# wq loaded ahead of the transposes, and k and q of each tile in turn, in a gated mix of linear attention and a GeGLU FFN

## The chip, the cores and the metric

The kernel runs on one core of one Trainium2 chip. The metric is the device time of one execution in microseconds (us). A profiled execution also leaves a trace, whose span, from the first to the last instruction, is 1.2 to 1.5 us shorter than the time in nearly every run. SP and ACT name the queues of SyncE and ScalarE, from which the loads are issued. "Landing" below is the moment at which the last of the 16 DMA engines reports a load complete, read from the trace's landing records.

## The reference, cut to what matters

S = 2048 rows, D = 640, F = 1728, 32 heads of 20.

```python
g = sigmoid((x * gate_w).sum(-1, keepdims=True))
q, k, v = split(x @ wqkv)                        # 32 heads of 20
pq, pk = phi(q), phi(k)                          # phi(t) = where(t > 0, t + 1, exp(t)) + 1e-6
kv, z = einsum(pk, v), pk summed over the rows
a = (pq @ kv) / (pq @ z + 1e-6) @ wo
b = (gelu(x @ w_gate) * (x @ w_up)) @ w_down
out = g * a + (1 - g) * b
```

The change touches only the K/Q stage at the start: k = x wk and q = x wq for 16 tiles of 128 rows, followed by phi. A unit below is the k or the q of one tile: five pairs of matmuls (512 and 128 columns), one pair for each 128-row chunk of the weight (wk0 to wk4 are the chunks of wk, x0 and x1 the first tiles of x). The stage has 32 units, that is 160 pairs. After it comes the product of pk with x, "the pk^T x stage", then the FFN and the output, none of which the change touches.

## The kernel before

x is needed transposed. The first three tiles are loaded plainly and transposed on TensorE (T); the other 13 come through DMA transposes. `P.op` records an operation with what it reads and writes, and semaphore waits follow from that. `seq` gives the order of the units; `slot(n)` gives each unit a pair of PSUM banks (`ps` in the lines of the profile, where the matmuls write) in turn, four pairs in all.

```python
NXN, KLEAD = 3, 7
load_x(0, "sp");  load_wk(0, "act"); load_wk(1, "sp"); load_x(1, "act"); load_x(2, "sp")
load_wk(2, "act"); load_wk(3, "sp"); load_wk(4, "act"); # ... gate weights on "act"
for i in range(NXN, NT):
    if i == KLEAD:
        dma_in(wq[:, :, 0:640], ...)             # all of wq, behind four transposes
    load_xT(i, after=([r_wk[1]] if i == NXN else ()))
# ...
seq = [("k", i) for i in range(KLEAD)] + [("q", 0)]
for i in range(KLEAD, NT):
    seq += [("q", i - KLEAD + 1), ("k", i)]
seq += [("q", i) for i in range(NT - KLEAD + 1, NT)]
# ...
warm(6, 512)                                     # matmuls on constants, to warm the array
T(0, [0], 7); T(0, [1, 2, 3, 4], 6)              # transposes of tile 0, copied back by VectorE
KM(0, [0]); T(1, [0, 1, 2, 3, 4], 7); KM(0, [1]); warm(2, 128)
KM(1, [0]); KM(1, [1]); T(2, [0, 1, 2, 3, 4], 6)
# ... chunk 2 of k0 and k1, chunks 0 to 2 of k2; gate_col() transposes the gate weights
for k in range(3, KC):
    for n in range(3):
        KM(n, [k])                               # three k tiles by chunk
for n in range(2 * NT):                          # the rest, unit by unit
    if seq[n][0] == "q": QM(n)
    elif n >= 3:         KM(n, list(range(KC)))
    phi1(n); phi2(n)                             # Exp on ScalarE, two VectorE operations
```

## Time and profile before

| | before |
|---|---|
| time, median of 3 runs | 276.66 us (276.47 to 277.04) |
| span of the trace | 275.2 us |
| PE busy | 271.3 us, 99% of the span |
| first transpose | 4.17 us |
| first k product | 4.72 us |
| first q product | 16.08 us |
| first product of the pk^T x stage | 50.11 us |

From the page of the kernel before: the busy time of TensorE (first its matmuls, then its weight loads, VectorE and ScalarE), the array's clock in 40 slices, and the chain of work that ended last.

```profile
PE 271.3 (99%) x1694; PEld 139.3 (51%) x1694; DVE 138.8 (50%) x234; ACT 78.3 (28%) x132; POOL 26.1 (9%) x28
...
PEclk9999999999999999999999999999999999999999
...
PE 96%; DMA 1%; DVE 1%; ACT 0%; issue 0%
```

TensorE bounds the kernel almost from end to end, so what a new order of loads and tiles can win lies in its first microseconds. The chain of waits cut off at 20 us shows them, as start, length and what (lines that are plain runs of matmuls are left out):

```profile
0.81 3.32 DMA pool<-in_A_x_dram
...
4.44 0.24 DVE pool L419
...
5.49 0.50 DVE pool L419
...
10.02 0.71 ACT pool L462
10.75 0.34 DVE pool L472
11.12 0.84 DVE pool L476
```

The chain begins with the load of x tile 0, then alternates between TensorE and VectorE's copies of transposes, and at 10 us passes once through phi of unit 0: unit 4 needs the banks of unit 0. The timeline of TensorE gives the rate (start, duration, engine, line, operation, and in brackets the idle time before and what ended it):

```profile
0.84 2.72 PE L401 MATMUL ps<-const-bfloat16-1.0 128*128 128x512 bf16 x6 [0.84 <-PEq L818]
4.17 0.45 PE L415 MATMUL ps<-pool 128*128 128x128 bf16 x5 [0.61 <-DMA pool<-in_A_x_dram]
4.72 0.39 PE L438 MATMUL ps<-pool 128*128 128x512 bf16 x1
4.95 0.22 PE L439 MATMUL ps<-pool 128*128 128x128 bf16 x1
...
16.08 0.38 PE L453 MATMUL ps<-pool 128*128 128x512 bf16 x1
```

Two speeds are to be seen. The six warm matmuls of 512 columns take 0.43 us each (start to start); from 4.17 us on a pair of 512 and 128 columns takes 0.39 and 0.22 us, overlapping, and in a row a pair starts every 0.272 us.

### The profile page before, as it was taken

What the parts mean: (1) busy time and instruction counts of PE and PEld (TensorE: products, weight loads), DVE (VectorE), ACT (ScalarE), POOL (GpSimd) and SP (SyncE); (2) the same over time, 40 slices, a digit from 0 to 9 for tenths busy, and PEclk for the clock granted to TensorE, in tenths of its full rate; (3) what the DMA queues carried; (4) which work ended last, traced back from release to release, by engine and by line L of the source; (5) the groups of instructions that cost most, each with busy time, mean ns of one, the idle gap of its engine ahead of it and who ended that gap; (6) DMA issues with size and microseconds to landing.
All of it is one profiled execution on the core that took longest, in us unless ns stands there. A gap on an engine that the chain in (4) does not pass through costs nothing.

```text
span 275.2 us, 4067 instructions
## 1 busy us (share of the span) xinstructions
PE 271.3 (99%) x1694; PEld 139.3 (51%) x1694; DVE 138.8 (50%) x234; ACT 78.3 (28%) x132; POOL 26.1 (9%) x28
## 2 busy tenths in 40 slices
PE   7999999999999999999999999999999999999997
PEld 3555555555545444444444444444555555555553
DVE  1598888510234324999999999535100122212223
ACT  1455555210421454223322223224555100000000
POOL 5000000000000401242433422000000000000000
PEclk9999999999999999999999999999999999999999
DMA  6797999001121111122121231380000011111111
GB/s 206 164 181 176 388 403 311 15 11 39 24 48 22 50 46 53 26 46 48 26 49 24 48 45 29 67 304 14 0 0 2 15 42 40 48 50 48 50 40 55
DMA packets 36400, 22.38 MB, mean 81 GB/s; under 512 B 25759, under 2 KB 34975, under 8 KB 36383
## 3 DMA queue, kind: packets, MB, share of 16 engines
q1 hardware_dynamic: 35797, 21.47, 28.3%
q10 hardware_dynamic: 586, 0.66, 0.8%
q8 instruction: 13, 0.21, 0.3%
q14 instruction: 4, 0.03, 0.0%
HBM read 13.11 MB, written 2.62 MB: 57 GB/s over the span
## 4 chain that ended last, share of the span: by engine, by line
PE 96%; DMA 1%; DVE 1%; ACT 0%; issue 0%
PE ps L623 41%; PE ps L766 20%; PE ps L530 6%; PE ps L729 6%; PE ps L453 6%; PE ps L438 6%; PE ps L454 2%; PE ps L532 2%; PE ps L730 2%; PE ps L598 2%; PE ps L439 1%; DMA pool<-in_A_x_dram 1%; PE ps L750 1%; PE ps L644 1%; PE ps L660 1%; DVE pool L777 0%
## 5 line engine op out<-in xcount | busy, mean ns | idle before, releaser
L623 PE MATMUL ps<-pool 128*128 128x512 bf16 x520 | 113.7, 379 | 0.0
L623 PEld LDWEIGHTS ps<-pool 128*128 128x128 bf16 x520 | 50.4, 98 | 60.0 <-issue 0.3
L766 PE MATMUL ps<-pool 128*128 128x512 bf16 (+1 forms) x416 | 57.2, 299 | 0.0
L631 DVE TENSOR_TENSOR pool<-ps,pool 128x512 bf16<-128x512 f32 x52 | 35.8, 688 | 33.5 <-PE ps L623 30.4
L629 ACT ACTIVATE pool<-ps 128x512 f32<-128x512 f32 x52 | 31.1, 597 | 72.5 <-PE ps L623 72.5
L777 DVE SCALAR_TENSOR_TENSOR pool<-ps,pool 128x512 bf16<-128x512 f32 (+1 forms) x32 | 16.2, 547 | 63.8 <-PE ps L766 63.8
L766 PEld LDWEIGHTS ps<-pool 128*128 128x128 bf16 x416 | 31.9, 98 | 25.2 <-issue 1.1
L675 POOL TENSOR_TENSOR pool<-pool 128x640 f32<-128x640 bf16 x16 | 22.5, 1408 | 139.7 <-DMA pool<-z_row 86.6
L462 ACT ACTIVATE pool<-ps 128x640 bf16<-128x640 f32 x32 | 22.3, 704 | 23.2 <-PE ps L439 13.0
L476 DVE SCALAR_TENSOR_TENSOR pool<-ps,pool 128x640 bf16<-128x640 f32 x32 | 26.4, 825 | 2.2
L438 PE MATMUL ps<-pool 128*128 128x512 bf16 x80 | 23.5, 380 | 0.5 <-DVE pool L419 0.2
L683 DVE TENSOR_TENSOR pool<-pool 128x640 bf16<-128x640 bf16 x16 | 23.0, 1440 | 0.6
L453 PE MATMUL ps<-pool 128*128 128x512 bf16 x80 | 22.9, 379 | 0.0
L530 PE MATMUL ps<-pool 128*128 128x512 bf16 x80 | 21.9, 379 | 0.0
L729 PE MATMUL ps<-pool 128*128 128x512 bf16 x80 | 21.8, 379 | 0.0
L454 PE MATMUL ps<-pool 128*128 128x129 bf16 x80 | 17.6, 220 | 0.0
L532 PE MATMUL ps<-pool 128*128 128x129 bf16 x80 | 17.6, 220 | 0.0
L439 PE MATMUL ps<-pool 128*128 128x128 bf16 x80 | 17.5, 219 | 0.0
L730 PE MATMUL ps<-pool 128*128 128x128 bf16 x80 | 17.5, 219 | 0.0
L734 ACT ACTIVATE pool<-ps,pool 128x640 f32<-128x640 f32 x16 | 12.7, 794 | 9.2 <-PE ps L730 9.2
L677 DVE TENSOR_REDUCE pool<-pool 128x32 f32<-128x640 f32 x16 | 13.0, 810 | 0.0
L438 PEld LDWEIGHTS ps<-pool 128*128 128x128 bf16 x80 | 7.8, 98 | 10.1 <-DVE pool L419 1.0
(51 smaller groups left out, 125.7 us busy)
## 6 DMA issues: line engine op xcount, KB each, us to landing
out_dram<-pool SPq DMA_DIRECT2D x15, 160.0 KB, 1.8
pool<-in_B_w_gate_dram SPq DMA_DIRECT2D x1, 2080.0 KB, 14.1
pool<-in_B_w_up_dram SPq DMA_DIRECT2D x1, 2080.0 KB, 18.8
pool<-in_A_wqkv_dram SPq DMA_DIRECT2D x2, 800.0 KB, 11.8
pool<-in_A_x_dram SPq DMA_DIRECT2D x1, 1280.0 KB, 8.7
pool<-in_B_w_down_dram SPq DMA_DIRECT2D x1, 1120.0 KB, 6.0
pool<-in_A_wo_dram SPq DMA_DIRECT2D x6, 160.0 KB, 9.0
pool<-in_B_w_down_dram SPq DMA_DIRECT2D x1, 960.0 KB, 8.1
```

Source lines behind the costliest of these rows:

```text
L438: e.matmul(ps[:, b0, :], lhs, wk[:, k, 0:512], start=(k == 0), stop=(k == KC - 1))
L453: e.matmul(ps[:, b0, :], lhs, wq[:, k, 0:512], start=(k == 0), stop=(k == KC - 1))
L454: last = e.matmul(ps[:, b1, 0:129], lhs, wq[:, k, 512:641], start=(k == 0), stop=(k == KC - 1))
L476: P.op("dve", lambda e: e.scalar_tensor_tensor(dst, ps_flat[:, b0 * 512:b0 * 512 + 640], 1.0 + EPS, e_buf[m], ALU.add, ALU.max), reads=[ba ...
L530: e.matmul(ps[:, bs[n], :], lhs, x_aug[:, i, 0:512], start=(i == 0), stop=(i == NT - 1))
L532: last = e.matmul(ps[:, bt, n * 129:(n + 1) * 129], lhs, x_aug[:, i, 512:641], start=(i == 0 and n == 0), stop=(i == NT - 1), skip_group_c ...
L623: last = e.matmul(ps[:, b, :], w[:, k, fc * 128:(fc + 1) * 128], xT[:, k, j * 512:(j + 1) * 512], start=(k == 0), stop=(k == KC - 1))
L629: P.op("act", lambda e: e.activation(ge[n], ps[:, gb, :], ACT.Gelu_apprx_tanh), reads=[bank[gb]], writes=[r_ge[n]])
L631: P.op("dve", lambda e: e.tensor_tensor(hT[fc][:, j * 512:(j + 1) * 512], ps[:, ub, :], ge[n], ALU.mult), reads=[bank[ub], r_ge[n]], write ...
L729: e.matmul(ps[:, b0, :], lhs, w2[:, m, 0:512], start=(m == 0), stop=(m == KC - 1))
L730: last = e.matmul(ps[:, b1, 0:128], lhs, w2[:, m, 512:640], start=(m == 0), stop=(m == KC - 1))
L766: last = e.matmul(dst, lhs, wd[:, fc, c0:c0 + cn], start=False, stop=(fc == NFC - 2), skip_group_check=True)
```

## The change

The intent: have wq there early, so that q of a tile can follow its k at once and only two tiles need transposing on TensorE; let four units (k0, k1, q0, q1) consume the weights chunk by chunk as they land; then take k and q of each tile in turn, which needs a new transposed tile only every 2.7 us.

```diff
-NXN = 3
-KLEAD = 7
+NXN = 2
-            load_x(0, "sp"); load_wk(0, "act"); load_wk(1, "sp"); load_x(1, "act"); load_x(2, "sp")
-            load_wk(2, "act"); load_wk(3, "sp"); load_wk(4, "act"); gate weights on "act"
+            gate weights on "act"
+            load_x(0); load_wk(0); load_x(1, "act"); load_wk(1); load_wk(3)      # default queue: SP
+            P.op("act", lambda e: e.activation(eg[:, 0:1], zero, ACT.Exp), ...)  # early table load
+            load_wk(2, "act"); load_wk(4, "act")
+            load_wq(0, 2); load_wq(2, KC, "act")
             for i in range(NXN, NT):
-                if i == KLEAD: dma_in(wq[:, :, 0:640], ...)
-                load_xT(i, after=([r_wk[1]] if i == NXN else ()))
+                load_xT(i, after=([r_wk[4]] if i == NXN else ()))
 # ... (cut: resources of the two first tiles; QM takes a list of chunks)
+            seq = [("k", 0), ("k", 1), ("q", 0), ("q", 1)]
+            for i in range(2, NT):
+                seq += [("k", i), ("q", i)]
-            warm(6, 512) ... three tiles by chunk, as shown above
+            warm(5, 512); warm(1, 128)
+            T(0, [0], 7); T(0, [1, 2, 3, 4], 6); warm(3, 128); KM(0, [0])
+            T(1, [0], 7); T(1, [1, 2, 3, 4], 6); warm(3, 128); KM(1, [0])
+            for k in (1, 3): KM(0, [k]); KM(1, [k])
+            gate_col()
+            for k in (2, 4): KM(0, [k]); KM(1, [k])
+            # then q0 and q1 by chunk: QM(2, [k]); QM(3, [k]) for k = 0, 1, 2, then [3, 4]; then unit by unit
```

(The diff is cut, and lines are joined.)

More of the change, by code (lines that the diff above doesn't have):

```diff
@@ L300, in bass_gated_mix__linear_attn_block__geglu_ffn__prompt_kernel @@
             r_xT = [P.sb("xT%d" % i, R_XT, R_XT + KC * S) for i in range(NT)]
-            r_x0a = P.sb("x0a", R_XT, R_XT + 128)
+            r_xTa = [P.sb("xTa%d" % i, R_XT, R_XT + S) for i in range(NXN)]
             r_wk = [P.sb("wk%d" % k, R_WK + k * 640, R_WK + (k + 1) * 640) for k in range(KC)]
@@ L341, in load_wk, with load_x, load_wq @@
                 dma_in(wk[:, k, :], A_wqkv[k * 128:(k + 1) * 128, 640:1280], [r_wk[k]], eng=eng)
-            load_x(0, "sp")
-            load_wk(0, "act")
-            load_wk(1, "sp")
+            def load_x(i, eng="sp"):
+                dma_in(x_aug[:, i, 0:640], A_x[0, i * 128:(i + 1) * 128, :], [r_xn[i]], eng=eng)
+            def load_wk(k, eng="sp"):
+                dma_in(wk[:, k, :], A_wqkv[k * 128:(k + 1) * 128, 640:1280], [r_wk[k]], eng=eng)
+            def load_wq(k0, k1, eng="sp"):
+                dma_in(wq[:, k0:k1, 0:640],
+                       A_wqkv[k0 * 128:k1 * 128, 0:640].rearrange("(k p) w -> p k w", p=128),
+                       r_wq[k0:k1], eng=eng)
+            dma_in(gw_sb[0:5, :], gate_w.rearrange("(k p) -> k p", p=128), [r_gw], eng="act")
+            load_x(0)
+            load_wk(0)
             load_x(1, "act")
-            load_x(2, "sp")
+            load_wk(1)
+            load_wk(3)
+            zero = nc.const_aps.tensor(0.0, (128, 1), F32)
+            P.op("act", lambda e: e.activation(eg[:, 0:1], zero, ACT.Exp), writes=[r_eg[0]])
             load_wk(2, "act")
-            load_wk(3, "sp")
             load_wk(4, "act")
-            dma_in(gw_sb[0:5, :], gate_w.rearrange("(k p) -> k p", p=128), [r_gw], eng="act")
+            load_wq(0, 2)
+            load_wq(2, KC, "act")
             def load_xT(i, after=()):
@@ L358, in bass_gated_mix__linear_attn_block__geglu_ffn__prompt_kernel @@
             for i in range(NXN, NT):
-                if i == KLEAD:
-                    dma_in(wq[:, :, 0:640], A_wqkv[:, 0:640].rearrange("(k p) w -> p k w", p=128), r_wq)
-                load_xT(i, after=([r_wk[1]] if i == NXN else ()))
+                load_xT(i, after=([r_wk[4]] if i == NXN else ()))
             dma_in(x_aug[:, NXN:8, 0:640],
@@ L408, in slot @@
             def slot(n):
-                return SLOTS[n] if n < 3 else SLOTS[n % 4]
+                return SLOTS[n % 4]
             def T(i, ks, tb):
@@ L421, in T @@
                     psb[:, tb, 0:len(ks) * 128].rearrange("p (k s) -> p k s", k=len(ks))),
-                    reads=[bank[tb]], writes=[r_x0a if i == 0 and ks[0] == 0 else r_xT[i]])
-            seq = [("k", i) for i in range(KLEAD)] + [("q", 0)]
-            for i in range(KLEAD, NT):
-                seq += [("q", i - KLEAD + 1), ("k", i)]
-            seq += [("q", i) for i in range(NT - KLEAD + 1, NT)]
+                    reads=[bank[tb]], writes=[r_xTa[i] if ks[0] == 0 else r_xT[i]])
+            seq = [("k", 0), ("k", 1), ("q", 0), ("q", 1)]
+            for i in range(2, NT):
+                seq += [("k", i), ("q", i)]
             def KM(n, ks):
@@ L441, in fn, with QM @@
                     return last
-                P.op("pe", fn, reads=[r_x0a if i == 0 and ks == [0] else r_xT[i]] + [r_wk[k] for k in ks],
+                P.op("pe", fn, reads=[r_xTa[i] if i < NXN and ks == [0] else r_xT[i]] + [r_wk[k] for k in ks],
                      writes=[bank[b0], bank[b1]])
-            def QM(n):
+            def QM(n, ks):
                 i = seq[n][1]
@@ L450, in fn @@
                     last = None
-                    for k in range(KC):
+                    for k in ks:
                         lhs = xT[:, k, i * 128:(i + 1) * 128]
@@ L456, in fn @@
                     return last
-                P.op("pe", fn, reads=[r_xT[i], r_gcol] + r_wq, writes=[bank[b0], bank[b1]])
+                P.op("pe", fn, reads=[r_xT[i], r_gcol] + [r_wq[k] for k in ks],
+                     writes=[bank[b0], bank[b1]])
             def phi1(n):
@@ L485, in gate_col @@
                      reads=[bank[7]], writes=[r_gcol])
-            warm(6, 512)
+            ALLK = list(range(KC))
+            warm(5, 512)
+            warm(1, 128)
             T(0, [0], 7)
             T(0, [1, 2, 3, 4], 6)
+            warm(3, 128)
             KM(0, [0])
-            T(1, [0, 1, 2, 3, 4], 7)
-            KM(0, [1])
-            warm(2, 128)
+            T(1, [0], 7)
+            T(1, [1, 2, 3, 4], 6)
+            warm(3, 128)
             KM(1, [0])
-            KM(1, [1])
-            T(2, [0, 1, 2, 3, 4], 6)
-            KM(0, [2])
-            KM(1, [2])
-            KM(2, [0])
-            KM(2, [1])
-            KM(2, [2])
+            for k in (1, 3):
+                KM(0, [k])
+                KM(1, [k])
             gate_col()
-            for k in range(3, KC):
-                for n in range(3):
-                    KM(n, [k])
+            for k in (2, 4):
+                KM(0, [k])
+                KM(1, [k])
             for n in range(2 * NT):
-                if seq[n][0] == "q":
-                    QM(n)
-                elif n >= 3:
-                    KM(n, list(range(KC)))
+                if n == 2:
+                    for k in range(3):
+                        QM(2, [k])
+                        QM(3, [k])
+                    QM(2, [3, 4])
+                    QM(3, [3, 4])
+                elif n > 3:
+                    (KM if seq[n][0] == "k" else QM)(n, ALLK)
                 phi1(n)
                 phi2(n)
-                if n == 6:
+                if n == 8:
                     late_constants()
```

## The prediction

> **What bounds the kernel now.** TensorE. The page has PE busy 271.3 of 275.2 us, and the chain of waits is 96% PE. In the steady part of the K/Q stage a 512+128 matmul pair starts every 0.272 us (timeline); 160 such pairs are 43.6 us. The stage runs from the first transpose at 4.17 us, which waited for x tile 0 (0.61 us by the waits view), to the first pk^T x matmul at 50.11 us: 45.9 us. Only 2.4 us of it, plus the start before 4.17 us, can be won.
>
> Where the 2.4 us lie (timeline, 4.17 to 16.08 us, 35 pairs = 9.5 us of 11.9): transposes and the copy to the first product 0.55; transposes of tiles 1 and 2 and two warm matmuls about 0.8; holes at 5.8 to 6.0 and 7.4 to 7.7 us behind the copies of transposes; gate transpose 0.3; 0.34 before the fourth K tile at 12.00 us, which waits for the first phi to free its banks.
>
> **What the change does.**
> 1. x0 now is alone at the head of the SP queue; only a 1.2 KB load precedes x1 on ACT's. Before, x0 shared the engines with wk0 and landed at 3.9 to 4.1 us. [...]together they move about 360 KB per us here. Estimate: x0 (164 KB) lands at 3.4 to 3.8 us, saving 0.3 to 0.7 us.
> 2. One tile fewer by PE transpose: about 0.35 us of PE and one hole of 0.2 to 0.3 us saved. More small warm matmuls (seven of 128 instead of two) take 0.1 to 0.3 us back.
> 3. Four accumulators (k0, k1, q0, q1) run before a slot is needed again, so the 0.34 us bank wait goes.
> 4. Added: the early Exp pulls the table load (1.28 us) ahead of wk2 and wk4 on ACT; these land about 1 us later (estimate 6.0 and 7.0 us), which is why chunk 3 precedes 2. PE reaches chunk 2 at about 6.9, so at most 0.3 us of new wait.
> 5. wq (820 KB) ahead of the transposes: x0, x1, wk and wq are 1.97 MB, about 5.5 us at that rate; all landed by about 8.3 us, needed between 8.0 and 9.1. The DMA transposes wait for wk4, first issue about 7 instead of 4.84 us, first tile about 10.3 us (3.5 us from issue to landing before); needed at about 10.7. After that tiles arrive every 1.3 us and are used every 2.72, so no stall.
>
> **Sum.** Four units end at about 10.7 us, 28 more at 1.362 us each end at about 48.9 us: the pk^T x stage starts 1.2 us earlier on the PE chain. Allowing for small waits I take 1.1 us: 276.66 becomes **275.5 us** (-0.4%), 8 in 10 between 274.4 and 276.5. Chances: faster by over 2% 0.01, within 2% 0.98, slower by over 2% 0.01.
>
> **What would show it.** In the timeline: first transpose at 3.4 to 3.8 us; first pk^T x matmul at 48.6 to 49.5; no DVE wait near 12 us; no PE wait on DMA transposes; from there to the end both traces equal in length (225 us).
>
> **What would make it wrong.** x0 landing no earlier (gain about 0.6); wk2/wk4 landing after 7.5 us because ACT's table load holds its queue longer (PE stalls, up to 1 us, and the transposes start late behind it); the first DMA-transposed tile after 11 us; the array clock falling back to half rate in an early wait (the six warm matmuls took 0.45 us each).

("They" are the two queues: in the profile before, the core's DMA engines moved 387 KB from 3 to 4 us and 356 KB from 4 to 5 us. 10.7 and 28 times 1.362 us come to 48.8, put there as 48.9, 1.2 us before 50.11, of which 1.1 were taken.)

## The result, and the profile after

| | before | after |
|---|---|---|
| time, median of 6 runs each | 276.79 us (276.47 to 277.04) | 276.21 us (275.65 to 277.09) |
| ratio, 95% interval | | 0.9982 (0.9964 to 1.0001) |
| span of the trace | 275.2 us | 274.9 us |
| first transpose | 4.17 us | 3.12 us |
| first k product | 4.72 us | 4.49 us |
| first q product | 16.08 us | 9.01 us |
| first product of the pk^T x stage | 50.11 us | 49.82 us |

A ratio is the mean time of one kernel's fast runs over that of the other's of the same rounds, so it is not quite the ratio of the medians quoted. The gain is 0.2%, less than half of the predicted 0.4%. Two later jobs timed the same kernel again at 0.9986 (0.9974 to 0.9998) and 0.9977 (0.9964 to 0.9991): three jobs, 0.14 to 0.23%, that is 0.4 to 0.6 us in place of 1.1. The interval of the first job alone just includes no gain; those of the two later ones do not.

From the page after, the same lines:

```profile
PE 271.7 (99%) x1693; PEld 140.3 (51%) x1693; DVE 138.5 (50%) x234; ACT 78.5 (29%) x133; POOL 26.1 (9%) x28
...
PEclk9999999999999999999999999999999999999999
...
PE 97%; DMA 1%; DVE 0%; SPq 0%; issue 0%
```

The chain of waits up to 14 us, its first lines:

```profile
0.81 0.39 SPq L332
1.20 0.06 issue
1.26 3.10 DMA pool<-in_A_wqkv_dram
4.35 0.14 issue
4.49 0.59 PE ps L451
...
5.18 0.53 PE ps L429 x5
```

And TensorE's timeline:

```profile
0.84 2.40 PE L415 MATMUL ps<-const-bfloat16-1.0 128*128 128x512 bf16 x6 [0.84 <-PEq L836]
3.12 0.71 PE L429 MATMUL ps<-pool 128*128 128x128 bf16 x5
...
4.49 0.59 PE L451 MATMUL ps<-pool 128*128 128x512 bf16 x1 [0.34 <-DMA pool<-in_A_wqkv_dram]
4.87 0.31 PE L452 MATMUL ps<-pool 128*128 128x128 bf16 x1
...
5.83 0.63 PE L451 MATMUL ps<-pool 128*128 128x512 bf16 x1
...
6.69 0.22 PE L452 MATMUL ps<-pool 128*128 128x128 bf16 x1
6.74 0.38 PE L451 MATMUL ps<-pool 128*128 128x512 bf16 x1
...
7.76 0.39 PE L451 MATMUL ps<-pool 128*128 128x512 bf16 x1
...
8.59 0.38 PE L451 MATMUL ps<-pool 128*128 128x512 bf16 x1
8.80 0.22 PE L452 MATMUL ps<-pool 128*128 128x128 bf16 x1
9.01 0.38 PE L466 MATMUL ps<-pool 128*128 128x512 bf16 x1
```

Three things are to be seen. The chain no longer starts with x0 but with wk0, which landed at 4.35 us: x0 was there at 3.07 and the first transpose ran 1.05 us earlier than before, but the first product only 0.23 us earlier. Until 6.6 us the matmuls have the half-rate durations (0.59 to 0.63, 0.31, and 0.71 for five transposes, against 0.45). And between the last k product and the first q product there is a gap: the matmul of 512 columns before the last 128 one started at 8.59, a pair takes 0.272, so the q product was due at 8.86 and started at 9.01. The first part of wq (chunks 0 and 1) landed at 8.87.

From the first q product on nothing moves. Its distance to the pk^T x stage is 40.81 us, and from there the trace lasts 225.1 us as before (275.2 less 50.11, 274.9 less 49.82). So the question is why the first q product came at 9.01 us and not at 8.0: the prediction had four units end at 10.7 us, and q0 and q1 are ten pairs of 0.272 us, which puts their start at 8.0.

### The profile page after: what moved, and what is told of

It is laid out like the page before. It is cut to its first block, busy times and chain, and to the rows that moved or that the text cites. A ratio compares the mean times of both kernels' runs of the same rounds, so it can differ in the third digit from the quotient of the medians.

```text
span 274.9 us, 4067 instructions
## 1 busy us (share of the span) xinstructions
PE 271.7 (99%) x1693; PEld 140.3 (51%) x1693; DVE 138.5 (50%) x234; ACT 78.5 (29%) x133; POOL 26.1 (9%) x28
## 4 chain that ended last, share of the span: by engine, by line
PE 97%; DMA 1%; DVE 0%; SPq 0%; issue 0%
PE ps L641 41%; PE ps L784 20%; PE ps L451 7%; PE ps L466 6%; PE ps L747 6%; PE ps L548 6%; PE ps L452 2%; PE ps L550 2%; PE ps L467 2%; PE ps L748 2%; PE ps L616 2%; DMA pool<-in_A_wqkv_dram 1%; PE ps L768 1%; PE ps L662 1%; PE ps L678 1%; DVE pool L795 0%
## 5 line engine op out<-in xcount | busy, mean ns | idle before, releaser
L486 DVE TENSOR_SCALAR pool<-pool 128x640 bf16<-128x640 bf16 x32 | 10.4, 326 | 5.3 <-ACT pool L476 4.1
```

## The experiments

Two theories stood at the start. **Clock**: the array stayed at half rate up to 6.6 us, where the profile before had happened to be at full rate from 3.9 us. **Loads**: the products wait for wk0, x1 and wq, which land later than reckoned, whatever the clock. The key figures of all profiles are here, worked out from the timeline and the landing records. "Full rate" is where the durations change. The two intervals are from the issue of x0 to the first q product and to the first product of the pk^T x stage; x0 is issued at 0.80 or 0.81 us except in the runs named pw (pre-warmed: matmuls on constants run before the first load).

```
run            full rate  wk0 landed  wq, first part  first q   x0 issue to q   x0 issue to pk^T x
before            3.9        3.92        15.06         16.08       15.27            49.30
look_before_1     5.6        3.75        15.08         16.35       15.54            49.57
pw_before      before x0   x0+3.17     x0+14.33       21.29       15.00            49.03
after             6.6        4.35         8.87          9.01        8.20            49.01
look_after_1      5.0        3.98         9.51          9.65        8.85            49.66
after_again       6.5        4.54         8.71          8.93        8.13            48.95
after_3           6.8        3.90         8.62          8.76        7.96            48.77
pw_after       before x0   x0+3.04      x0+7.89        14.86        8.03            48.84
nowq            4.1-4.8       4.64          -            8.25        7.45            48.35
pw_nowq        before x0   x0+4.20         -           15.18        7.81            48.72
pw_nowq_2      before x0   x0+3.89         -           14.08        7.50            48.40
hold_t            5.5        4.29         8.50          8.63        7.83            49.52
wk0_act           5.1        4.35         6.57*         8.64        7.84            48.66
after_plus        8.6        5.09         7.45         10.05        9.25            50.07
inorder           5.6        3.70         7.88          8.11        7.31            48.54
inorder_2         5.9        4.05         7.73          8.29        7.49            48.50
pw_inorder     before x0   x0+2.67      x0+6.86        14.68        7.15            48.63
kfirst            9.6        4.38        17.57         17.73       16.92            50.95
kfirst_fill       4.4        4.47        17.91         18.04       17.24            52.94
```

(After: chunks 0 and 1 of wq, one transfer. In after_plus and the inorder runs chunk 0 alone. *In wk0_act wq's first part had one load fewer ahead of it on SP's queue; that this brought it forward is not shown.)

### Full rate before the first load: pw_before and pw_after

```diff
+            def pw(e): 18 matmuls of 512 columns on constants
+            P.op("pe", pw, writes=[bank[4], r_pw])
-            first load on each queue
+            first load on each queue, reads=[r_pw]      # waits for the 18 matmuls
-            warm(6, 512)            # after: warm(5, 512)
+            warm(10, 512)
```

> Kernel before, with 18 warm matmuls of 512 columns ahead of everything and the first loads waiting for them, so that the array is at full rate before the first load is issued. Measured from the issue of x tile 0 to the first pk^T x matmul (49.30 us in the plain kernel). Clock theory and load theory agree here: the plain profile was at full rate from 3.86 us, before its first transpose, so 49.0 to 49.3 us.

> Changed kernel with the same 18 warm matmuls ahead of everything. Same interval, 49.01 us in the plain changed kernel. Clock theory (the lost 0.8 us is the array's half rate up to 6.6 us): 48.0 to 48.4 us, 0.9 to 1.2 below pw_before. Load theory (wk0 and x1 landing at 4.4 and 4.9 us hold the first products whatever the clock): 48.8 to 49.0 us, 0.3 below pw_before.

Measured: 49.03 and 48.84 us (one look each). The total times, 281.86 and 282.03 us, contain the added matmuls and mean nothing. The pure clock theory falls: with full rate from the start the changed kernel gains 0.17 us on itself, not the 0.6 to 1.0 of that theory, and is only 0.19 below pw_before. (The plain profiles of the changed kernel below spread from 48.77 to 49.66, so a difference of 0.2 is not to be told from none.) What it meets instead is in its waits of TensorE:

```profile
PE ps L463 <- DMA pool<-in_A_wqkv_dram: 0.6, 1, 0.6
PE ps L477 <- DMA pool<-in_A_wqkv_dram: 0.3, 1, 0.3
```

L463 is a k product that waits for wk1 (the record of the 512-column matmul before it is missing; from its usual place the wait itself was about 0.4 us), L477 the first q product. Faster products only arrived earlier at loads that were not there.

### The same kernels again: look_before_1, look_after_1, after_again, after_3

No edit.

> The kernel before again, to see whether the moment at which the array goes to full rate moves from run to run. If it is fixed by the program: 3.8 to 3.9 us again, span 275.2. If its phase is free[...]: [...]a late moment costs up to 1 us of span.

> The changed kernel again. Fixed by the program: full rate from 6.5 to 6.6 us and span 274.9 again. Free phase: another moment, [...]with a span of 274.0 to 274.3 if it is before 4 us.

> The changed kernel on the same chip as the three others, for the size of the change: 276.0 to 276.5 us, 0.997 to 0.999 of before. In its trace the first q product to the first pk^T x product is 40.81 us again, so that the time moves only with the first q product (9.0 and 9.65 us before).

> The changed kernel beside inorder on one chip: 276.0 to 276.3 us, 0.998 to 0.999 of before.

Measured: full rate came at about 5.6 us in look_before_1, where the profile before had 3.9, and at 5.0, 6.5 and 6.8 us in the three others. The moment is not fixed by the program. But a late moment did not cost what was expected: look_before_1 lost 0.27 us, and look_after_1, at full rate earlier than the first profile, was the slowest of the four (276.84 us, first q product at 9.65). Its chain of waits up to 14 us and its waits of TensorE say why:

```profile
2.67 6.84 DMA pool<-in_A_wqkv_dram
9.51 0.14 issue
9.65 0.38 PE ps L466
```

```profile
PE ps L466 <- DMA pool<-in_A_wqkv_dram: 0.7, 1, 0.7
PE ps L451 <- DMA pool<-in_A_wqkv_dram: 0.5, 2, 0.3
```

Here the chain starts with wq. In the profile after and in after_again it starts with wk0. In after_3, where wk0 landed at 3.90, it is TensorE alone from its first warm matmul, much of it at half rate. Set against the landing of wq's first part, the first q product started 0.14 us later in after, look_after_1, after_3 and pw_after (9.01 for 8.87, 9.65 for 9.51, 8.76 for 8.62, 14.86 for 14.72), and 0.22 us later in after_again. In three of the four plain profiles TensorE itself was ready for it within 0.22 us of that moment (8.86 in after; 8.93 in after_again and 8.76 in after_3 with no gap before it); in look_after_1 it was ready at 8.81. So there are two limits of nearly equal size, the chain of k products, stretched by half rate, and the landing of wq. The expectation of 40.81 us from the first q product to the pk^T x stage held in all four profiles.

### No wq load: nowq, pw_nowq, pw_nowq_2

A wrong result: q products read wk in place of wq (relative error 0.045), so that they wait for no load and 820 KB are not moved.

```diff
-            load_wq(0, 2)
-            load_wq(2, KC, "act")
-   e.matmul(ps[:, b0, :], lhs, wq[:, k, 0:512], ...)      # and wq[:, k, 512:641]
+   e.matmul(ps[:, b0, :], lhs, wk[:, min(k, 3), 0:512], ...)   # and 129 columns of wk
```

> Changed kernel without the load of wq; the q products read wk instead (wrong result on purpose), so the first q product waits for no load. Steady part unchanged. If wq's landing alone sets the first q product (9.0 and 9.65 us in the two plain profiles): it starts at 8.0 to 8.4 us and the pk^T x stage at 48.8 to 49.2. If the half-rate clock, or the landing of wk, is a second limit of nearly the same size: 8.5 to 9.0 us and 49.3 to 49.8, with no wait just before the first q product; the exact value moves with the moment of full rate.

> Both suspects taken away: full rate before the first load is issued, and no wq load (wrong result on purpose). From the issue of x0 to the first q product: 8.20 us in the plain changed profile, 8.03 with full rate alone. Two-limits theory: 7.0 to 7.5 us, and first pk^T x product 47.8 to 48.3 us after the issue. If the landings of wk hold the products even so: 7.6 to 8.0.

> pw_nowq again, whose wk0 had one engine 1.3 us behind the others. Without such a tail: from the issue of x0 to the first q product 6.9 to 7.4 us, against 8.03 in pw_after (full rate, but wq's landing waited for) and 7.45 in nowq (wq not loaded, half rate up to 4.7 us).

Measured: nowq 8.25 us for the first q product and 275.63 us median of 4 (275.26 to 278.25; ratio 0.9985, interval 0.9944 to 1.0026 with the one run at 278.25 in it, so the time alone shows nothing). By its figures nowq met the expectation of wq's landing as the only limit (8.25 us and 49.15). But its profile was also lucky in the clock, full rate by 4.8 us, so it removes both limits at once and cannot tell the theories apart; wq removed at a late full rate was not measured. Together they are worth 0.76 us at the first q product (9.01 less 8.25). The two pw looks, with full rate for certain, were no better: 7.81 and 7.50 us from the issue of x0, because wk0 came late, 4.20 and 3.89 us after that issue. In pw_nowq_2 TensorE stood 1.06 us before the first k product:

```profile
10.60 0.38 PE L460 MATMUL ps<-pool 128*128 128x512 bf16 x1 [1.06 <-DMA pool<-in_A_wqkv_dram]
```

So behind the two limits stands a third, wk0. The 6.9 to 7.4 us expected of both removals was missed for that reason.

nowq also gives the price of half rate. From the first k product to chunk 2 of k0 (same instructions, no wait for a load in between in any of them) it took 2.38 us (4.77 to 7.15) where after took 3.27 (4.49 to 7.76), after_again 3.15 (4.68 to 7.83) and after_3, at half rate the longest, 3.63 (4.03 to 7.66): 0.8 to 1.2 us. TensorE's timeline of nowq:

```profile
4.77 0.38 PE L449 MATMUL ps<-pool 128*128 128x512 bf16 x1 [0.62 <-DMA pool<-in_A_wqkv_dram]
...
7.15 0.39 PE L449 MATMUL ps<-pool 128*128 128x512 bf16 x1
...
8.25 0.38 PE L464 MATMUL ps<-pool 128*128 128x512 bf16 x1
```

And of after_3:

```profile
4.03 0.58 PE L451 MATMUL ps<-pool 128*128 128x512 bf16 x1
...
7.66 0.39 PE L451 MATMUL ps<-pool 128*128 128x512 bf16 x1
...
8.76 0.38 PE L466 MATMUL ps<-pool 128*128 128x512 bf16 x1
```

### Transposes held back: hold_t

```diff
-  load_xT(i, after=([r_wk[4]] if i == NXN else ()))
+  load_xT(i, after=([r_wk[4]] + r_wq if i == NXN else ()))
```

> Changed kernel, with the DMA transposes held until wq has landed too. If the transposes, issued at 6.6 us, are what stretches the landing of wq's first part (7.8 us median of its engines, 8.9 the last): its last engine lands by 7.9 us. If it is only the bytes queued before it: 8.4 to 9 us again. Either way the first DMA-transposed tile comes after 12 us and K tile 2 waits about 1 us for it, so this one is no faster in total.

Measured (one look): wq's first part landed at 8.50 us, its second at 9.12, against 8.62 to 9.51 and 9.28 to 10.30 in the four plain profiles. The transposes are not the main cause. That leaves the bytes queued ahead, which no run varied alone. K tile 2 then waited 0.72 us for the first DMA-transposed tile, as expected, and the time was 276.70 us.

### wk0 on the other queue: wk0_act

```diff
-            load_wk(0)
+            load_wk(0, "act")
```

> One part of the load order undone: wk0 on ACT's queue again, sharing the engines with x0. If the later of x0 and wk0 sets the first product: x0 lands at 3.9 to 4.2 us, wk0 at 3.6 to 4.0, first transpose about 4.1, first k product at 4.5 to 4.8 us as in the changed kernel (4.49, 4.12), time within 0.3 us of it. If x0's early landing by itself is worth the 0.5 us that was predicted: first k product 0.5 to 1 us later than the changed kernel's, and so the time.

A half miss: x0 still landed at 3.13 us. The gate weights ahead of wk0 on ACT's queue take 0.57 us to issue, so wk0 was issued at 1.39 us and x0 again at 0.80. wk0 landed at 4.35 and the first k product came at 4.48, as in the changed kernel; the time, 276.25 us (0.9988, interval 0.9975 to 1.0001), is the changed kernel's of the same job, 276.07 (0.9986). It doesn't tell the worth of x0's early landing; it does say that moving wk0 to the other queue, behind those weights, makes no difference.

### The old tile order with the new load order: kfirst, kfirst_fill

```diff
 # on the kernel before
-            loads of before
+            gate weights on "act"; x0, wk0, wk1, wk3 on SP; x1, x2, wk2, wk4 on "act"
-  load_xT(i, after=([r_wk[1]] if i == NXN else ()))
+  load_xT(i, after=([r_wk[3]] if i == NXN else ()))
-            for k in range(3, KC):
-                for n in range(3):
-                    KM(n, [k])
+            for n in range(3):
+                KM(n, [3, 4])
-            warm(6, 512)
+            warm(5, 512); warm(1, 128)
 # kfirst_fill: also warm(8, 128) before KM(0, [0]) and warm(5, 128) after T(1, ...)
```

> A candidate: the tile order of the kernel before (seven k first, three tiles by PE transposes, wq among the DMA transposes, so q waits for no load), with only the load order of the change (x0, wk0, wk1, wk3 on SP; gate weights, x1, x2, wk2, wk4 on ACT) and chunks 3 and 4 of each of the three first tiles together, so that the first phi starts 1 us earlier and frees its banks. If the loads of wq were what cost the changed kernel its gain: first transpose at 3.1 us, no bank wait near 12 us, first pk^T x matmul at 48.8 to 49.3 us, 275.5 to 275.9 us, faster than both. If the clock or the wk landings cost it: 49.5 to 50.0, 276.2 to 276.6.

> kfirst, which stayed at half rate up to 9.6 us and took 277.9 us, with 8 and 5 more warm matmuls of 128 columns in its two holes (before the first k product, and after the transposes of tile 1). Clock theory[...]: full rate by 6.6 us, first pk^T x product by 50.3 us, time 276.0 to 276.6. If the delay of kfirst comes from its loads: full rate no earlier, 277.5 us or more.

Neither met an expectation in full, and both were slower than either kernel: kfirst 277.86 us (1.0044, interval 1.0026 to 1.0063), kfirst_fill 279.41 us (1.0104, interval 1.0072 to 1.0136). As a candidate and as a test of the loads kfirst was badly made: holding the transposes for wk3 pushed wq, which sits among them, to 17.57 us. In kfirst this was hidden, as the array stayed at half rate up to 9.6 us, with holes of 0.65 and 0.55 us in TensorE's work. With those holes filled full rate came at 4.4 us, within the expected 6.6. As its moment moves by itself from run to run and these are single profiles, that the filling did it is not shown. TensorE then ran out of work at 15.8 us and waited for wq. TensorE's timeline of kfirst_fill:

```profile
15.37 0.38 PE L438 MATMUL ps<-pool 128*128 128x512 bf16 x1
15.58 0.22 PE L439 MATMUL ps<-pool 128*128 128x128 bf16 x1
18.04 0.59 PE L453 MATMUL ps<-pool 128*128 128x512 bf16 x1 [2.24 <-DMA pool<-in_A_wqkv_dram]
...
21.10 0.32 PE L454 MATMUL ps<-pool 128*128 128x129 bf16 x1
...
21.57 0.22 PE L454 MATMUL ps<-pool 128*128 128x129 bf16 x1
```

One wait of 2.24 us cost more than itself: the matmuls after it have half-rate durations again (0.59 to 0.63 us from 18.04 to 20.67, 0.38 from 21.62 on), and the page's clock row has a 7 in its third slice (13.9 to 20.9 us). Not every execution fell back: of its four runs two were at a mean clock of 0.994 (280.30 and 280.85 us) and two at 1.000 (278.03 and 278.53). As in the start of the changed kernel, behind one limit stood the other.

### Mended versions: after_plus, inorder, inorder_2, pw_inorder

after_plus moves the gate transpose into the wait for wk0, loads wq as four transfers, so that the first q product needs chunk 0 alone, and has two more warm matmuls. inorder also puts the eleven early loads of x, wk and wq on SP's queue in the order of need (the gate weights stay on ACT's), and takes the chunks in that order.

```diff
 # after_plus, on the changed kernel
-            load_wq(0, 2); load_wq(2, KC, "act")
+            load_wq(0, 1); load_wq(1, 2); load_wq(2, 3, "act"); load_wq(3, KC, "act")
-            warm(3, 128); KM(0, [0])                  # gate_col() taken out below
+            gate_col(); warm(5, 128); KM(0, [0])
 # inorder, on after_plus
-            load_x(0); load_wk(0); load_x(1, "act"); load_wk(1); load_wk(3); ...
+            x0, wk0, x1, wk1, wk2, wk3, wk4, wq0, wq1, wq2, wq3-4, all on SP
-            for k in (1, 3): ...  for k in (2, 4): ...
+            for k in (1, 2): ...  for k in (3, 4): ...
```

> The changed kernel mended where the traces show waits: gate transpose moved into the wait for wk0 (0.25 us off the chain), wq loaded as four transfers so that the first q product waits for chunk 0 alone, two more warm matmuls. If wq's landing and the chain before it both limit: first q product at 8.2 to 8.7 us, first pk^T x product at 49.0 to 49.6, 275.5 to 276.0 us, 0.3 to 0.7 faster than the changed kernel. If only the DMA engines' late tails count: no better than 276.2.

> The changed kernel with all twelve early loads on one queue in the order in which the array needs them (x0, wk0, x1, wk1 to wk4, wq0 to wq4), the gate transpose in the wait for wk0. If sharing the 16 engines between two queues is what delays wk0 (4.35 and 4.54 us in the changed kernel) and wq's first part (8.9, 9.5, 8.7): wk0 lands by 3.8 us, wq chunk 0 by 7.0, first q product at 7.6 to 8.3, first pk^T x product at 48.4 to 49.1, 275.0 to 275.6 us, whatever the moment of full rate up to 0.9 us. If the clock alone is the limit: first q product at 8.3 us or later and 275.7 or more.

> The same with the array at full rate before the first load is issued. From the issue of x0 to the first q product: 8.03 us in pw_after. Two-limits theory: with both limits gone 6.5 to 7.2 us. Loads alone: no shorter than in inorder, 7.0 to 7.5. Clock alone: same as pw_after, 8.

> inorder again, beside the changed kernel: 275.6 to 275.9 us, 0.996 to 0.9975 of before, 0.2 to 0.5 us below the changed kernel, and less spread from run to run than it, because the loads arrive in order of need and half rate early on then hides behind them. If its first result was luck of the chip or of the moment of full rate: within 0.1 us of the changed kernel.

Measured: after_plus 275.87 us median of 6 (0.9978, interval 0.9964 to 0.9991), four runs at 275.55 to 276.00 and two at 276.80 and 277.31. The last of these was profiled: wk0 landed at 5.09 and full rate came at 8.6 us, so its first q product, at 10.05, missed the expected 8.2 to 8.7. inorder 275.74 us (275.69 to 275.86; 0.9967, interval 0.9954 to 0.9981), the steadiest of all; its first q product came at 8.11 us, wk0 at 3.70. The first q product was within the expectation, the time (275.0 to 275.6) was not. In the second job, beside the changed kernel, it was 275.97 (0.9973, interval 0.9960 to 0.9985), the changed kernel 275.97 (0.9977). The means differ by 0.1 us (275.93 and 276.03), so inorder beats the kernel before, but that it beats the changed kernel, by 0.2 to 0.5 us as expected, is not shown.

On the cause they say this. From the issue of x0 to the first q product pw_inorder took 7.15 us and pw_after 8.03: at full rate both, so 0.88 us came without the clock. It came from the edit as a whole (the order, the queue, the smaller first part of wq and the gate transpose moved), not from the order alone, which no run isolates. And inorder, at half rate up to 5.6 us, took 7.31, so that full rate gave it only 0.16 more. The 7.15 rules out the clock as the only limit, but it fits the loads alone (7.0 to 7.5) as well as two limits (6.5 to 7.2). inorder gives part of this back: from the first q product to the pk^T x stage it took 41.23 us in place of 40.81, waiting for the last chunks of wq, which landed at 10.04 us. The pw pair gives most of it back: to the pk^T x stage it is 48.63 against 48.84. TensorE's timeline of inorder:

```profile
8.11 0.38 PE L466 MATMUL ps<-pool 128*128 128x512 bf16 x1
...
10.08 0.39 PE L466 MATMUL ps<-pool 128*128 128x512 bf16 x1 [0.17 <-DMA pool<-in_A_wqkv_dram]
```

Even with both limits removed, no run came below 48.35 us from x0's issue to the pk^T x stage; the prediction had 48.1 (48.9 less 0.8).

## Why the prediction was wrong

The mechanism and the sign were right and the time lies within the range, but the size was off by a factor of two or more. The term of the sum that was mis-sized is "Four units end at about 10.7 us". In the profile after they ended at 11.73 us (the first q product at 9.01 and ten pairs of 0.272). The rest of the sum held: 28 units of 1.362 us from there give 49.9, and the pk^T x stage began at 49.82. Point by point:

- **Only the start can be won, and what is won there survives.** Right. The rest lasts 225.1 us in both traces, and the first q product to the pk^T x stage is 40.81 us in every profile of the changed kernel. The wait for phi's banks at 12 us is gone.
- **"x0 (164 KB) lands at 3.4 to 3.8 us, saving 0.3 to 0.7 us."** It landed even earlier, at 3.07, and the first transpose gained 1.05 us. The saving did not follow: the first product needs wk0 too, which landed at 4.35, 3.98, 4.54 and 3.90 us in the four plain profiles, against 3.92 and 3.75 before. x0 landed 1.06 us sooner than before (3.07 for 4.13), wk0 0.43 later (4.35 for 3.92), and the last of x0, wk0 and x1 no sooner (4.79 for 4.56). With the new order on two queues (profiles that start cold) wk0 landed at 3.90 to 5.09 us, in order on one queue at 3.70 and 4.05. The sum never asked when wk0 lands.
- **"these land about 1 us later"** (wk2 and wk4, held by the table load). Wrong but harmless: ACT issued wk2 at 1.86 us, beside the table load at 1.80 to 3.08, and the two landed at 5.69 and 6.59.
- **"all landed by about 8.3 us, needed between 8.0 and 9.1."** This is the first half of the step that failed, in size. The estimate divided 1.97 MB by 360 KB per us, near the best rate of the start before (387 and 356 KB in the microseconds from 3 and 4 us), and took the mean engine. wq's first part landed at 8.62 to 9.51 and its second at 9.28 to 10.30 us. The last engine counts, 0.7 to 1.4 us behind the median one in the four plain profiles (first part: 7.74 and 8.87 in after, 8.14 and 9.51 in look_after_1), and a first q product that waits for it starts 0.14 us after it.
- **"the array clock falling back to half rate in an early wait"** was named as a risk (such a fall was seen in kfirst_fill, behind a wait of 2.24 us), but the array never left half rate before 5.0 to 6.8 us. This is the other half of the failed step. "Four units end at about 10.7 us" silently took the full rate from 3.9 us of the one profile before. This costs 0.8 to 1.2 us of the chain of k products (nowq against after, after_again and after_3). It is not additional to the wait for wq: with the clock removed alone, 0.17 us came back in one look.
- **DMA transposes and steady state.** Right: the first tile landed at 10.37 us (10.3 predicted), and no plain profile shows a wait for one.

So of the 1.1 us expected, 0.4 to 0.6 came. The change turned a start that only TensorE and its copies bounded, with wq needed at 16 us and landed at 15, into one in which the k products, at half rate, and wq's landing both end at 8.6 to 9.5 us. In the order of after, look_after_1, after_again and after_3, the k products were done and TensorE ready for q at 8.86, 8.81 (with 0.5 us of waits for wk1 and wk3 in it), 8.93 and 8.76 us, 0.8 to 0.9 later than the 8.0 of the prediction; wq's landing then added 0.15, 0.84, 0 and 0. Had the k products been on time, wq's first part, landed at 8.62 to 9.51, would have held q about as long or longer. Shown: each of the two is a limit (look_after_1 and pw_after for the loads, after_3 and after_again for the chain), and the clock removed alone returned little in the one look taken. Not settled: how the missing 0.5 to 0.7 us divides on average over runs, since the moment of full rate (5.0 to 6.8 us in the four plain profiles) and the late engines move from run to run.

Between 3 and 4 us of the changed kernel SP's queue moved 0.15 MB and ACT's 0.16 MB, and their loads landed mixed (x0 and wk0 of SP at 3.07 and 4.35, x1 of ACT at 4.79, wk1 of SP at 5.28, wk2 of ACT at 5.69 us). That the two queues share the engines was used in the prediction only for the total rate, not for the order.

## What to carry to other kernels

In a start where loads and matmuls keep pace, list for each early product when the last engine of each of its operands lands; an operand that comes earlier gains little while its partner does not (here x0 came 1.06 us earlier, the first product 0.23). Early loads on one queue in the order of need are worth a trial: here that, with smaller first parts, brought the first q product forward (8.11 and 8.29 us against 8.76 to 9.65), though no gain in time over the changed kernel was shown. Before counting on a warm array take several profiles (here full rate came 2.8 to 8.8 us after the first matmul), and read the rate from the matmuls' own durations.

## What else the traces showed

- The moment of full rate: in the five pw runs, whose first matmuls follow each other without a hole, about 2.8 to 5.3 us after the first matmul (worked out from when the 18 matmuls ended: 0.43 us each at half rate, half of that at full rate). With holes in the work it came up to 8.8 us after it (kfirst), and for the changed kernel 4.2, 5.7, 5.7 and 6.0 us after it.
- Five transposes took 0.71 to 0.74 us while the matmuls were at half rate and 0.45 us at full rate: they follow the clock.
- In the first 10 us the last of the 16 engines of one load came up to 2.2 us behind the median (wk4 in look_after_1: 5.93 and 8.12 us; in the profile after at most 1.1, wq's first part: 7.74 and 8.87), and this is what waits see.
- The profile page's clock row does not show the start: it reads 9 in the first slice (0 to 6.9 us) of the changed kernel, where nearly all matmuls had half-rate durations. The trace's clock record begins at 6.58 us there.
